# Gathers of rows as four plain 32-row loads, in a transformer block with all its gradients

## The chip, the cores and the metric

The kernel runs on one core of a Trainium2 chip. The metric is the device time of one execution in microseconds (us); the time before is the median of three runs. One further execution was recorded by the hardware profiler; its trace gives every duration below. TensorE is called PE, VectorE DVE, ScalarE ACT, GpSimd POOL; SP is the engine that only issues transfers.

## What is computed

One transformer block, forward and backward, at S = 2048 rows, D = 512, 32 heads of 16 columns and F = 1792, all in bfloat16. Attention is local and dilated: each row sees eight rows of its own past, two apart.

```python
def _A_ref(x, wqkv, wo):
    qkv = (x @ wqkv).reshape(B, S, 3, H, Dh).transpose(2, 0, 3, 1, 4)
    q, k, v = qkv[0], qkv[1], qkv[2]
    idx = pos[:, None] - (jnp.arange(8) * 2)[None, :]          # masked where < 0
    kg, vg = k[:, :, idx], v[:, :, idx]
    attn = _softmax(jnp.where(mask, einsum("bhsd,bhswd->bhsw", q, kg) * scale, -1e9))
    o = einsum("bhsw,bhswd->bhsd", attn, vg)
    return o.transpose(0, 2, 1, 3).reshape(B, S, D) @ wo
h  = x + _A_ref(_layernorm(x), wqkv, wo)
h2 = h + (_gelu(_layernorm(h) @ w1 + b1) @ w2 + b2)
out = h2, and the gradients of x, wqkv, wo, w1, b1, w2, b2 for grad_out
```

## The kernel before

The rows are worked in four chunks (`NC = 4`) of `CH = 512`. The forward pass goes through layer norm, the products with wqkv, attention, wo, a second layer norm and the two MLP products; then come the MLP's backward products, attention's backward pass chunk by chunk, and the weight gradients, which are dense matmuls that fill PE wherever they are placed.

Attention is not done with matmuls of q and k, as each row has eight partners only. Scores come from `dots` (product at L422): DVE multiplies q by the eight shifted copies of k, 128x4096 elements at a time (`prf` forward, `prb` backward), and PE sums over the head's columns (L430). What is weighted and summed over the eight partners goes through `band` (product at L449): DVE multiplies a tile `R` of fetched rows by coefficients `cf` (`prbo` for the output, `prbq`, `prbk` and `prbv` for the gradients), PE sums (L458) and ACT scales the result (L463). One `R` serves four such products.

`R` is filled by `gather` (L406, its transfer at L411): each of 128 partitions gets 18 rows of 512 numbers that lie in one piece in device memory, 18,432 bytes, and 2.36 MB in all. The rows come from `v_d`, `k_d`, `q_d` or `go_d`, where transposed copies of v, k, q and of the gradient of o were stored before. There are sixteen gathers: `Ro` of v for the forward pass, and `Rq` of k, `Rv` of go and `Rk` of q for the backward pass, each once a chunk. A gather is one indirect transfer on GpSimd's queue; the table `rowi`, written by eight small GpSimd instructions at L323, holds the index of each partition's first row. The same queue carries the stores of o and of the gradients of q, k and v (L266), the mask, and `rstd` (L346), a power taken for the layer norms.

The program is recorded as a list of operations by the class `Plan`; `op` derives from the tiles read and written what must come before what. `emit` then writes them in the sequence of the table `ORDER`, with each tile at the address in the table `HOMES`. Both tables are the result of a planner, which gave every operation a cost; the costs in the calls of `op` do nothing in the finished program. Each engine takes its instructions strictly in the order written. A tile can be loaded only when the tile that had its address is no longer read: in the backward pass `Rk`, `Rq` and `Rv` of one chunk can be issued only when the last product that reads the tile there has ended.

Three more places bear on the change. `consts` writes small constant matrices (`S32`, `Sum4`, `Pmat`, `Emat`), most on ACT. The layer norm of chunk 0 takes its root on ACT (L340, tile `ve`) and the reciprocal on DVE (L342). `warm` (L290) puts sixteen matmuls on a tile of zeros between PE's first products.

Of the kernel before, what the change touches and what calls it, by code (L numbers as in the profile page):

```python
# [10 lines left out]
P = 128  # L11
# [5 lines left out]
H = 32  # L17
# [131 lines left out]
def kernel(  # L149
# [43 lines left out]
    def cst(name, shape, dt=BF16):  # L193
# [8 lines left out]
    mhalf = cst("mhalf", [P, TPC], F32)  # L202
    epsc = cst("epsc", [P, 1], F32)
    zrow = cst("zrow", [RPAD, D])
    rowi = cst("rowi", [P, 2], mybir.dt.uint32)
# [28 lines left out]
    IDENT, PMAT, SUM4, NSUM4, S32B, SMB, IND8, EMAT, MKB, MHALF, ZROW, ROWI = (fx(n, None) for n in (  # L234
        "ident", "pmat", "sum4", "nsum4", "s32", "sm", "ind8", "emat", "mk", "mhalf", "zrow", "rowi"))
# [3 lines left out]
    EPSC = fx("epsc", epsc)  # L239
# [20 lines left out]
    def load(dst, ap, src_ap, kb, r=(), key=None, tag="load", soft=(), row=1, q="SP"):  # L260
        return op(q, 0.5, lambda: (SY if q == "SP" else A).dma_start(out=ap(), in_=src_ap()), r=r, w=[(dst, key)],
                  dma=kb / (DMA_RATE if row == 1 else WIDE_RATE), tag=tag, soft=soft, piece=0.006 + 0.0385 * row, mode=4)

    def store(dst, ap, src, src_ap, kb, key=None, skey=None, q="SP", tag="store", row=1):
        e, us = (SY, 0.45) if q == "SP" else (G, 0.6)
        return op(q, us, lambda: e.dma_start(out=ap(), in_=src_ap()), r=[(src, skey)], w=[(dst, key)] if dst is not None else (),  # L266
                  dma=kb / (DMA_RATE if row == 1 else WIDE_RATE), tag=tag, piece=0.006 + 0.0385 * row, mode=5)
# [14 lines left out]
    def warm(n):  # L282
# [8 lines left out]
        op("PE", 0.427 * n, mm, r=[z], w=[pz], tag="warm")  # L291

    def consts():
# [7 lines left out]
        op("ACT", 0.25, lambda: A.copy(out=_sub(Pmat[:], [[1, 8], [8, DH]]), in_=_sub(ident[:], [[DH, 8], [1, DH]])), r=[IDENT], w=[PMAT], tag="k")  # L301
        for j in range(4):
            op("ACT", 0.2, lambda j=j: A.copy(out=S32[32 * j:32 * j + 32, :], in_=ident[32 * j:32 * j + 32, 32 * j:32 * j + 32]),
               r=[IDENT], w=[(S32B, j)], tag="k")
# [10 lines left out]
        for g in range(4):  # L315
            op("ACT", 0.2, lambda g=g: A.copy(out=Emat[:, g, 8 * g:8 * g + 8], in_=ind8[:]), r=[IND8], w=[EMAT], tag="k")
# [88 lines left out]

    def gather(d_b, back, tag, soft=()):  # L406
        R = sb("R" + tag, [P, RW, 512])

        def g():
            t = d_b()  # L410
            G.indirect_dma_start(out=R().rearrange("p a d -> p (a d)"), out_offset=None,  # L411
                                 in_=_ap(t[0:1, :], [[RW * D, RB // RW], [1, RW * D]]),
                                 in_offset=bass.IndirectOffsetOnAxis(ap=rowi[:, int(back):int(back) + 1], axis=1),
                                 element_offset=(RPAD - 14 if back else 0) * D)
        op("POOL", 1.0, g, r=[d_b, ROWI], w=[R], dma=GATHER, tag="gather" + tag, soft=soft, piece=0.8, mode=4)
        return R
# [86 lines left out]
    wqk = sb("wqk", [P, DC, 2 * D])  # L503
    wv = sb("wv", [P, DC, D])
# [36 lines left out]
    def p1_proj(c, sel, dst, off, tag):  # L541
        for g2 in range(2):
            ps = ps_("psq" + tag, 2)
            for gg in range(2):
                g = 2 * g2 + gg

                for dcs in [range(DC)] if c in FM1 else [(0, 1), (2, 3)]:
                    def mm(g=g, gg=gg, ps=ps, dcs=dcs):
                        for dc in dcs:
                            T.matmul(ps()[:, gg * 512:(gg + 1) * 512], lhsT=wqk()[:, dc, sel * D + g * P:sel * D + (g + 1) * P],  # L550
                                     rhs=cols(st_[c]["ln1T"], dc, c in FM1), start=(dc == 0), stop=(dc == DC - 1))
                    op("PE", len(dcs) * MM, mm, r=[(wqk, sel), (st_[c]["ln1T"], None if c in FM1 else dcs[0] // 2)], w=[(ps, gg)], tag="qkv" + tag)
# [20 lines left out]
    def p1_qkv(c):  # L573
# [5 lines left out]
        else:  # L579
            kp = st_[c - 1]["kt"]  # L580
            op("DVE", 0.12, lambda: V.tensor_copy(out=kt()[:, :, 0:PAD], in_=kp()[:, :, CH:CH + PAD]), r=[(kp, 0), (kp, 1)], w=[(kt, "h")], tag="halo")
# [3 lines left out]
        to_tm_store(kt, PAD, k_d, c, True, "k", True)  # L585
        to_tm_store(qt, 0, q_d, c, False, "q", True)

    def p1_attn(c):
        d = st_[c]
        L = ps_("L", 2)  # L590
        dots(d["qt"], d["kt"], L, "f", lambda g: Emat[:, g, :], EMAT)
# [209 lines left out]
    def p3_go(c):  # L801
# [20 lines left out]
        to_tm_store(got, 0, go_d, c, False, "go", False)  # L822
# [175 lines left out]
    for i in (1, 0, 2):  # L998
        b = wv if i == 2 else wqk
        load(b, lambda b=b, i=i: b()[:, :, i % 2 * D:(i % 2 + 1) * D], lambda i=i: A_wqkv[:, i * D:(i + 1) * D].rearrange("(a p) j -> p a j", p=P), 512,  # L1000
             key=None if i == 2 else i, tag="wqkv")
    for c in range(1, NC):
# [106 lines left out]
FMB = ()  # L1109
LNK = 0  # L1110
# [167 lines left out]
```

## Time and profile before

| | us |
|---|---|
| three runs | 587.62, 597.37, 586.55 (median 587.62) |
| the profiled execution | 592.57 |
| its span | 590.8 |
| DVE busy | 494.9 |
| ACT busy | 379.1 |
| POOL busy | 45.7 |
| gathers, from issue to landing, median: Ro, Rq, Rv, Rk | 11.1, 10.7, 10.8, 11.8 |

The 1.8 us between span and time lie outside the recorded instructions. A row of the timeline gives the start and the length of a run of equal instructions, then engine, line, operation, the tiles written and read, and how many; in brackets stands how long the engine had been idle before and what ended that. `x4` in a row of 9 us is four instructions on end. PE's clock is shown as a share of full speed in each stretch; a matmul at half the clock takes twice as long and still counts as busy.

### The profile page before, as it was taken

What the parts mean: (1) busy time and instruction counts of PE and PEld (TensorE: products, weight loads), DVE (VectorE), ACT (ScalarE), POOL (GpSimd) and SP (SyncE); (2) the same over time, 40 slices, a digit from 0 to 9 for tenths busy, and PEclk for the clock granted to TensorE, in tenths of its full rate; (3) what the DMA queues carried; (4) which work ended last, traced back from release to release, by engine and by line L of the source; (5) the groups of instructions that cost most, each with busy time, mean ns of one, the idle gap of its engine ahead of it and who ended that gap; (6) DMA issues with size and microseconds to landing.
All of it is one profiled execution on the core that took longest, in us unless ns stands there. A gap on an engine that the chain in (4) does not pass through costs nothing. (4 is left out here: it accounts for less than half of the span.)

```text
span 590.8 us, 9131 instructions
## 1 busy us (share of the span) xinstructions
PE 555.7 (94%) x3526; PEld 265.3 (45%) x3580; DVE 494.9 (84%) x656; ACT 379.1 (64%) x549; POOL 45.7 (8%) x48
## 2 busy tenths in 40 slices
PE   3889997999999999999999999999999999969996
PEld 1444543455444444444444444455444444424442
DVE  7849979999999989959968878889989788768933
ACT  5878878999899973868913564552447743732622
POOL 1110021010000000000000200000110100701000
PEclk9989998999999999999999999999999999988999
DMA  8379886997642356469698998899989989274233
GB/s 262 103 235 299 239 316 178 289 206 223 159 120 78 99 148 184 116 136 225 132 182 166 197 195 211 256 285 227 312 278 263 311 256 349 66 313 161 63 99 98
DMA packets 160459, 118.68 MB, mean 201 GB/s; under 512 B 112480, under 2 KB 156064, under 8 KB 158368
## 3 DMA queue, kind: packets, MB, share of 16 engines
q1 hardware_dynamic: 157104, 76.68, 52.8%
q0 software_dynamic: 3312, 41.42, 19.4%
q8 instruction: 28, 0.46, 0.3%
q14 instruction: 15, 0.12, 0.1%
HBM read 55.74 MB, written 35.60 MB: 155 GB/s over the span
## 5 line engine op out<-in xcount | busy, mean ns | idle before, releaser
L779 PE MATMUL ps<-goT,w2T 128*128 128x512 bf16 x224 | 54.2, 379 | 0.0
L697 PE MATMUL ps<-ln2T,w 128*128 128x512 bf16 x224 | 52.6, 379 | 0.6 <-ACT xb L699 0.4
L793 PE MATMUL ps<-w1T,xb 128*128 128x512 bf16 x218 | 51.2, 379 | 0.3
L751 PE MATMUL ps<-w,gl 128*128 128x512 bf16 x218 | 50.5, 379 | 0.8 <-ACT gl L702 0.5
L781 DVE SCALAR_TENSOR_TENSOR xb<-xb,ps 128x512 bf16<-128x512 bf16 x56 | 37.0, 683 | 16.2 <-PE ps L779 11.6
L449 DVE TENSOR_TENSOR prbk<-Rk,cfk 128x4096 bf16<-128x4096 bf16 x16 | 35.8, 2287 | 14.5 <-issue 9.1
L907 PE MATMUL ps<-wqkvT,gqkvT 128*128 128x512 bf16 x187 | 45.8, 384 | 0.5 <-issue 0.3
L276 ACT CAST wgs<-ps 128x512 bf16<-128x512 f32 (+1 forms) x30 | 16.4, 558 | 46.5 <-PE ps L933 45.2
L699 ACT ACTIVATE xb<-ps,b1c 128x512 bf16<-128x512 f32 x56 | 35.9, 697 | 11.3 <-PE ps L697 8.5
L422 DVE TENSOR_TENSOR prb<-got,vw 128x4096 bf16<-128x4096 bf16 x16 | 36.1, 2282 | 7.8 <-PE ps L430 5.2
L933 PE MATMUL ps<-gw1in,ln 128*128 128x512 bf16 (+1 forms) x186 | 39.2, 352 | 0.3
L449 DVE TENSOR_TENSOR prbo<-Ro,cfo 128x4096 bf16<-128x4096 bf16 x16 | 36.0, 2282 | 3.6 <-DMA Ro<-v_d,rowi 3.6
L933 PE MATMUL ps<-gor,gw2in 128*128 128x512 bf16 x160 | 38.5, 379 | 0.5 <-issue 0.3
L276 ACT COPY gqkvT<-ps 128x1024 bf16<-128x1024 bf16 x24 | 23.8, 1014 | 20.2 <-PE ps L474 17.8
L422 DVE TENSOR_TENSOR prf<-qt,kt 128x4096 bf16<-128x4096 bf16 x16 | 35.8, 2276 | 1.1 <-ACT qt L276 1.1
L449 DVE TENSOR_TENSOR prbq<-Rq,cfq 128x4096 bf16<-128x4096 bf16 x16 | 35.7, 2282 | 1.1 <-PE ps L458 1.1
L449 DVE TENSOR_TENSOR prbv<-Rv,cfv 128x4096 bf16<-128x4096 bf16 x16 | 35.6, 2282 | 1.0 <-DMA Rv<-go_d,rowi 1.0
L933 PEld LDWEIGHTS <-ln 128*128 128x128 bf16 x256 | 24.4, 98 | 24.0 <-issue 2.5
L779 PEld LDWEIGHTS <-w2T 128*128 128x128 bf16 x224 | 21.8, 98 | 26.4 <-issue 0.4
L721 ACT ACTIVATE xb<-xb 128x2048 bf16<-128x2048 bf16 (+1 forms) x16 | 27.1, 1698 | 10.2 <-DVE xb L720 10.2
L793 PEld LDWEIGHTS <-xb 128*128 128x128 bf16 x224 | 21.8, 98 | 26.3 <-issue 0.2
L751 PEld LDWEIGHTS <-gl 128*128 128x128 bf16 x224 | 21.6, 98 | 26.5 <-ACT gl L702 1.2
(187 smaller groups left out, 1077.0 us busy)
## 6 DMA issues: line engine op xcount, KB each, us to landing
g_d<-gl SPq DMA_DIRECT2D x9, 512.0 KB, 4.6
gh_d<-xb SPq DMA_DIRECT2D x9, 512.0 KB, 3.4
w<-in_B_w_dram SPq DMA_DIRECT2D x2, 1792.0 KB
out_dram<-wgs SPq DMA_DIRECT2D x13, 256.0 KB, 4.7
xp<-in_A_x_dram SPq DMA_DIRECT2D x16, 128.0 KB, 3.6
ln_d<-ln SPq DMA_DIRECT2D x4, 512.0 KB, 6.2
gor<-in_grad_out_dram SPq DMA_DIRECT2D x16, 128.0 KB, 3.7
v_d<-tmv SPq DMA_DIRECT2D x8, 256.0 KB, 5.2
```

Of the source, the lines that this page charges most:

```text
L276: fn = lambda: A.copy(out=ap(), in_=pap())
L422: op("DVE", tt_us(4096), lambda g=g, pr=pr: V.tensor_tensor(out=pr(), in0=ql()[:, g, :].unsqueeze(1).to_broadcast([P, W, 512]), in1=_sub(k ...
L449: V.tensor_tensor(out=pr().rearrange("p a j (d h) -> p a j d h", h=H), in0=_sub(R()[:, o0, 0:1], [[st, 2], [512, 4], [32, DH], [1, H]]), i ...
L697: T.matmul(ps(), lhsT=w1()[:, dc, f * P:(f + 1) * P], rhs=cols(ln2T[c], dc, c in FM2), start=(dc == 0), stop=(dc == DC - 1))
L699: op("ACT", act_us(512, 1), lambda f=f, ps=ps, xb=xb, f0=f0: A.activation(out=xb()[:, f - f0, :], in_=ps(), func=ACT.Identity, bias=b1c[:, ...
L721: op("ACT", act_us(N), lambda xb=xb: A.activation(out=fl(xb), in_=fl(xb), func=ACT.Tanh, scale=GC), w=[xb], tag="tanh", mode=6)
L751: T.matmul(ps(), lhsT=d["g"][f // 4]()[:, f % 4, j * P:(j + 1) * P], rhs=w2()[:, f, :], start=(f == 0), stop=(f == FT - 1))
L779: T.matmul(ps(), lhsT=w2T()[:, dc, f * P:(f + 1) * P], rhs=cols(goT, dc, True), start=(dc == 0), stop=(dc == DC - 1))
L781: op("DVE", 0.61, lambda f=f, ps=ps, z=z, f0=f0: V.scalar_tensor_tensor(out=z()[:, f - f0, :], in0=z()[:, f - f0, :], scalar=1.0, in1=ps() ...
L793: T.matmul(ps(), lhsT=d["d"][f // 4]()[:, f % 4, j * P:(j + 1) * P], rhs=w1T()[:, f, :], start=(f == 0), stop=(f == FT - 1))
L907: T.matmul(ps(), lhsT=gT()[:, j, b * P:(b + 1) * P], rhs=wqkvT()[:, k0 + b, :], start=(i == 0 and b == 0), stop=(i == 2 and b == 3))
L933: T.matmul(ps()[:, 0:N], lhsT=l, rhs=r, start=(n == 0), stop=(n == k - 1))
```

## The change

In `gather`, the indirect transfer becomes four plain transfers of 32 partitions each, on the same queue. The source rows and the tile stay the same, so the table `rowi` and its eight instructions go. A product that reads the tile needs all four. In `consts`, ACT first takes the root of a constant, `sq0`, and the copies that make `Pmat`, `S32` and `Emat` come behind it, as they now read `sq0` as far as the planner sees; the ACT table loads fall from four to three. In `warm` the planner's cost alone is changed: the matmuls stay sixteen. Some options are added that are off (`QKP`, `TMD`). `ORDER` and `HOMES` are new from end to end: a new run of the planner over the changed list.

```diff
-        def g():
-            t = d_b()
-            G.indirect_dma_start(out=R().rearrange("p a d -> p (a d)"), out_offset=None,
-                                 in_=_ap(t[0:1, :], [[RW * D, RB // RW], [1, RW * D]]),
-                                 in_offset=bass.IndirectOffsetOnAxis(ap=rowi[:, int(back):int(back) + 1], axis=1),
-                                 element_offset=(RPAD - 14 if back else 0) * D)
-        op("POOL", 1.0, g, r=[d_b, ROWI], w=[R], dma=GATHER, tag="gather" + tag, soft=soft, piece=0.8, mode=4)
+        r0, dr = (RPAD - 2, -4) if back else (0, 4)
+        if GW == 4:
+            G_dma = lambda w: G.dma_start(out=R()[32 * w:32 * w + 32].rearrange("p a d -> p (a d)"), in_=_ap(d_b()[r0 + dr * w:r0 + dr * w + 1, :], [[16 * D, 32], [1, RW * D]]))
+            for w in range(4):
+                op("POOL", 0.58, lambda w=w: G_dma(w), r=[d_b], w=[(R, w)], dma=GATHER / 4, tag="gather" + tag, soft=soft, piece=0.8, mode=4)
...
-        op("PE", 0.427 * n, mm, r=[z], w=[pz], tag="warm")
+        op("PE", 0.2157 * n, mm, r=[z], w=[pz], tag="warm")
...
-        op("ACT", 0.25, lambda: A.copy(out=_sub(Pmat[:], [[1, 8], [8, DH]]), in_=_sub(ident[:], [[DH, 8], [1, DH]])), r=[IDENT], w=[PMAT], tag="k")
+        op("ACT", 0.25, lambda: A.activation(out=sq0[:], in_=epsc[:], func=ACT.Sqrt), r=[EPSC], w=[SQ0], tag="sd0", mode=7)
+        op("ACT", 0.25, lambda: A.copy(out=_sub(Pmat[:], [[1, 8], [8, DH]]), in_=_sub(ident[:], [[DH, 8], [1, DH]])), r=[IDENT, SQ0], w=[PMAT], tag="k")
...
-        for w4 in range(4):
-            for b_, o in ((0, 4 * w4), (1, 4 * (3 - w4))):
-                op("POOL", 0.12, lambda w4=w4, b_=b_, o=o: G.iota(rowi[32 * w4:32 * w4 + 32, b_:b_ + 1], pattern=[[0, 1]], base=o * D,
-                                                                 channel_multiplier=16 * D), w=[(ROWI, (w4, b_))], tag="k")
...
 ORDER = (
-    6, 14, 15, 13, 16, 7, 3, 17, 19, 20, 8, 5, 23, 24, 4, 0, 28, 11, 10, 82, 12, 2, 29, 35,
+    75, 6, 8, 11, 10, 5, 12, 24, 25, 26, 14, 42, 0, 7, 16, 3, 9, 60, 2, 52, 4, 48, 61, 62,
...
```

Three places of DVE's sequence show what the new tables do there. The numbers in a name are those of the tile's place in the list and its address; `st` and `mv` are a layer norm's statistics, `nm` its shift, `m` the maxima of the softmax, `jk` a dot product of the layer norm's backward pass (an `ISA` row, and one more that reads its sum), `gx` and `u` its results. Lines of the changed program lie 15 to 29 further down from the gather on (L449 is L464 there).

The first is DVE around the score products of chunk 0 and the maxima behind them. Before:

```order
L422 TENSOR_TENSOR prf_18_296<-qt_79_15_221,kt_19_3_123 128x4096
L581 COPY kt_121_18_303<-kt_19_3_123 128x4x16
L333 BN_STATS st<-xt_52_8_172 128x6
L334 BN_AGGR mv<-st 128x2
L422 TENSOR_TENSOR prf_19_308<-qt_79_15_221,kt_19_3_123 128x4096
L422 TENSOR_TENSOR prf_19_313<-qt_79_15_221,kt_19_3_123 128x4096
L422 TENSOR_TENSOR prf_20_315<-qt_79_15_221,kt_19_3_123 128x4096
L333 BN_STATS st<-xt_52_8_172 128x6
L334 BN_AGGR mv<-st 128x2
L344 TENSOR_SCALAR ve<-mv 128x4
L603 TENSOR_TENSOR m_153_18_409<-asb_16_401,ps 128x512
```

And now:

```order
L437 TENSOR_TENSOR prf_16_274<-qt_87_16_237,kt_0_1_99 128x4096
L346 SCALAR_TENSOR_TENSOR nm<-mv,rstd 128x4
L437 TENSOR_TENSOR prf_16_293<-qt_87_16_237,kt_0_1_99 128x4096
L437 TENSOR_TENSOR prf_17_296<-qt_87_16_237,kt_0_1_99 128x4096
L437 TENSOR_TENSOR prf_20_318<-qt_87_16_237,kt_0_1_99 128x4096
L330 BN_STATS st<-xt_78_14_222 128x6
L331 BN_AGGR mv<-st 128x2
L330 BN_STATS st<-xt_78_14_222 128x6
L331 BN_AGGR mv<-st 128x2
L330 BN_STATS st<-xt_78_14_222 128x6
L331 BN_AGGR mv<-st 128x2
L632 TENSOR_TENSOR m_148_17_394<-asb_16_382,ps 128x512
```

The four products `prf` now stand together, with one short `nm` between; the statistics of a tile that stood behind the first have moved away, and a third tile's statistics stand behind the last, ahead of `m`.

The second is DVE where the output products of the second `Ro` (`prbo`) meet the maxima of the next chunk's softmax (`m`). Before:

```order
L349 SCALAR_TENSOR_TENSOR nm<-mv,rstd 128x4
L449 TENSOR_TENSOR prbo_26_984<-Ro_28_820,cfo_26_957 128x4096
L603 TENSOR_TENSOR m_359_26_1014<-asb_25_1012,ps 128x512
L449 TENSOR_TENSOR prbo_26_1024<-Ro_28_820,cfo_26_957 128x4096
L605 TENSOR_TENSOR m_368_28_1030<-m_359_26_1014,m1h_27_1028 64x512
L449 TENSOR_TENSOR prbo_26_1034<-Ro_28_820,cfo_26_957 128x4096
L607 TENSOR_TENSOR m_382_23_1063<-m_368_28_1030,m2h_22_1061 32x512
L449 TENSOR_TENSOR prbo_22_1109<-Ro_28_820,cfo_26_957 128x4096
```

And now:

```order
L346 SCALAR_TENSOR_TENSOR nm<-mv,rstd 128x4
L632 TENSOR_TENSOR m_360_23_1009<-asb_22_1007,ps 128x512
L464 TENSOR_TENSOR prbo_22_1012<-Ro_29_867,cfo_21_974 128x4096
L634 TENSOR_TENSOR m_367_25_1023<-m_360_23_1009,m1h_24_1021 64x512
L464 TENSOR_TENSOR prbo_26_1044<-Ro_29_867,cfo_21_974 128x4096
L464 TENSOR_TENSOR prbo_24_1055<-Ro_29_867,cfo_21_974 128x4096
L636 TENSOR_TENSOR m_384_26_1065<-m_367_25_1023,m2h_25_1063 32x512
L464 TENSOR_TENSOR prbo_23_1073<-Ro_29_867,cfo_21_974 128x4096
```

The first `m` has moved from behind the first `prbo` to ahead of it; the last of the three stands behind the third product as before.

The third is DVE near the end of the backward pass, with the last product that reads one `Rq`, and `Rv` and `Rk` behind it. Before:

```order
L449 TENSOR_TENSOR prbq_36_4796<-Rq_35_4733,cfq_40_4424 128x4096
L1085 TENSOR_REDUCE gb_33_4855<-gb2p 128x4
L449 TENSOR_TENSOR prbv_34_4877<-Rv_33_4773,cfv_40_4352 128x4096
L449 TENSOR_TENSOR prbv_35_4898<-Rv_33_4773,cfv_40_4352 128x4096
L449 TENSOR_TENSOR prbv_35_4945<-Rv_33_4773,cfv_40_4352 128x4096
L449 TENSOR_TENSOR prbv_34_4970<-Rv_33_4773,cfv_40_4352 128x4096
L449 TENSOR_TENSOR prbk_34_4991<-Rk_36_4806,cfk_37_4520 128x4096
L449 TENSOR_TENSOR prbk_35_5011<-Rk_36_4806,cfk_37_4520 128x4096
L449 TENSOR_TENSOR prbk_35_5014<-Rk_36_4806,cfk_37_4520 128x4096
L495 ISA jk_1866_35_5041,sx<-gyr_1815_34_4857,ln1b_39_4540 128x512
L495 ISA sx 128x1
L449 TENSOR_TENSOR prbk_35_5043<-Rk_36_4806,cfk_37_4520 128x4096
```

And now:

```order
L464 TENSOR_TENSOR prbq_35_4825<-Rq_41_4694,cfq_40_4263 128x4096
L464 TENSOR_TENSOR prbv_33_4832<-Rv_41_4628,cfv_40_4428 128x4096
L510 ISA jk_1846_35_4878,sx<-gyr_1845_35_4876,ln1b_41_4539 128x512
L510 ISA sx 128x1
L510 ISA jk_1852_34_4894,sx<-gyr_1844_35_4874,ln1b_41_4539 128x512
L510 ISA sx 128x1
L464 TENSOR_TENSOR prbv_33_4951<-Rv_41_4628,cfv_40_4428 128x4096
L464 TENSOR_TENSOR prbv_34_4953<-Rv_41_4628,cfv_40_4428 128x4096
L464 TENSOR_TENSOR prbv_35_4966<-Rv_41_4628,cfv_40_4428 128x4096
L510 ISA jk_1875_34_4977,sx<-gyr_1845_35_4876,ln1b_41_4539 128x512
L510 ISA sx 128x1
L464 TENSOR_TENSOR prbk_36_4998<-Rk_33_4940,cfk_42_4681 128x4096
```

The products of `Rv` and `Rk` follow each other as before, but three `jk` now stand among or right behind the products of `Rv`, where there was none. On POOL's queue each gather's four parts stand together, but for one `Rv` near the end, whose last two parts stand behind all four of an `Rq`.

More of the change, by code (lines that the diff above doesn't have):

```diff
@@ L202 @@
     mhalf = cst("mhalf", [P, TPC], F32)
+    sq0 = cst("sq0", [P, 1], F32)
     epsc = cst("epsc", [P, 1], F32)
     zrow = cst("zrow", [RPAD, D])
[L205 removed]
     b1b = cst("b1b", [FT, P])
@@ L315, in consts @@
         for g in range(4):
-            op("ACT", 0.2, lambda g=g: A.copy(out=Emat[:, g, 8 * g:8 * g + 8], in_=ind8[:]), r=[IND8], w=[EMAT], tag="k")
+            op("ACT", 0.2, lambda g=g: A.copy(out=Emat[:, g, 8 * g:8 * g + 8], in_=ind8[:]), r=[IND8, SQ0], w=[EMAT], tag="k")
         op("POOL", 0.3, lambda: G.memset(mk[:], 0.0), w=[MKB], tag="k")
@@ L584, in p1_qkv @@
         p1_v(c)
-        to_tm_store(kt, PAD, k_d, c, True, "k", True)
-        to_tm_store(qt, 0, q_d, c, False, "q", True)
+        for fm, o, dd, back, n in ((kt, PAD, k_d, True, "k"), (qt, 0, q_d, False, "q")):
+            (tm_dma if (n, c) in TMD else to_tm_store)(fm, o, dd, c, back, n, c not in QKP)
     def p1_attn(c):
@@ L1001 @@
              key=None if i == 2 else i, tag="wqkv")
+    for i in (1, 0) if QKP else ():
+        op("POOL", 3.9, lambda i=i: G.tensor_copy(out=wqp()[:, :, i * D:(i + 1) * D].rearrange("p a (d h) -> p a d h", h=H),
+                                                  in_=_sub(wqk()[:, 0, 0:1], [[2 * D, DC], [1, DH], [DH, H]], i * D)), r=[(wqk, i)], w=[(wqp, i)], tag="hinwq")
     for c in range(1, NC):
@@ L1109 @@
 FMB = ()
+QKP = ()
+GW = 4
+TMD = ()
 LNK = 0
```

53 lines of the change are left out of this document (42 added, 11 removed), and 253 rows, old and new, of tables (HOMES, ORDER).

## The prediction

> **What bounds it now.** I read the page first: the busy shares and the slices.
>
> ```profile
> span 590.8 us, 9131 instructions
> PE 555.7 (94%) x3526; PEld 265.3 (45%) x3580; DVE 494.9 (84%) x656; ACT 379.1 (64%) x549; POOL 45.7 (8%) x48
> PE   3889997999999999999999999999999999969996
> PEclk9989998999999999999999999999999999988999
> ```
>
> PE is full nearly everywhere, and the change leaves its matmuls as they are. So what can be won is PE's idle time, 590.8 - 555.7 = 35.1 us, and the matmuls that run at a lower clock; the slices put both in the first sixth and in slices 36 and 37. What can be lost is not bounded in that way: DVE, at 84%, can become what PE waits for. The view of the waits then names what ends PE's idle time.
>
> ```profile
> PE ps L378 <- DVE ln L358: 8.6, 2, 7.7
> PE ps L458 <- DVE prbk L449: 6.8, 4, 3.0
> PE ps L400 <- ACT kt L276: 4.2, 1, 4.2
> PE ps L430 <- DVE prf L422: 2.7, 1, 2.7
> ```
>
> These four are 22.3 of the 35.1 us. The first is the start. The second is the late slices, where the timeline of the three engines, with POOL's rows first, shows the cause.
>
> ```profile
> 504.00 9.42 POOL L411 DMA_INDIRECT Rk<-q_d,rowi  x1 [11.83 <-DVE prbq L449]
> 513.73 0.94 POOL L411 DMA_INDIRECT Rv<-go_d,rowi  x1 [0.31 <-issue]
> 532.45 2.75 POOL L411 DMA_INDIRECT Rk<-q_d,rowi  x1 [17.78 <-DVE sx L495]
> ...
> 503.73 8.88 DVE L449 TENSOR_TENSOR prbv<-Rv,cfv 128x4096 bf16<-128x4096 bf16 x4
> 521.70 6.70 DVE L449 TENSOR_TENSOR prbk<-Rk,cfk 128x4096 bf16<-128x4096 bf16 x3 [9.09 <-issue]
> 528.32 0.68 DVE L495 CUSTOM_DVE_ANT_0 jk<-gyr,ln1b 128x512 bf16<-128x512 bf16 x1
> 532.10 6.69 DVE L449 TENSOR_TENSOR prbv<-Rv,cfv 128x4096 bf16<-128x4096 bf16 x3
> ...
> 526.25 0.61 PE L458 MATMUL ps<-prbk,S 128*32 128x512 bf16 x8 [3.00 <-DVE prbk L449]
> 528.45 1.89 PE L458 MATMUL ps<-prbk,S 128*32 128x512 bf16 x16 [1.59 <-DVE prbk L449]
> 531.39 1.04 PE L458 MATMUL ps<-prbk,S 128*32 128x512 bf16 x8 [1.04 <-DVE prbk L449]
> ```
>
> The issue of `Rk` takes 9.42 us, not the 0.94 of the next one. It begins 0.27 us into DVE's four `prbv` and ends at 513.42, 0.81 us behind their end at 512.61. The issue at 532.45 falls under the first of three `prbv` and lasts until 535.20, again 0.8 us behind that product's end (532.10 + 6.69 / 3 = 534.33). So while DVE runs such a product, the indirect issue stands still. The data then come late, DVE sits idle for 9.09 us, and PE waits three times, 5.63 us in all. A plain transfer on the same queue does not stand still: this store lies inside a run of such products.
>
> ```profile
> 425.77 0.58 POOL L266 DMA_DIRECT2D gv_d<-gvs  x1 [3.29 <-ACT gvs L463]
> ...
> 422.84 8.86 DVE L449 TENSOR_TENSOR prbq<-Rq,cfq 128x4096 bf16<-128x4096 bf16 x4
> ```
>
> [...]
>
> **The late bands.** The four issues of a gather take 4 x 0.58 = 2.3 us, 1.4 us more than 0.94, but start moving data after the first. With the stall gone, `Rk` at 504.00 would have been under way 8.5 us sooner, and DVE's 9.09 us would shrink to about one or two. In the new sequence the order of the parts here is `prbq`, four `prbv` with three `jk` among or behind them, then `prbk`; the parts of `Rk` can go out when the last `prbq` has ended, so DVE has 4 x 2.28 + 3 x 0.68, some 11 us of work before it needs them. The landing took this long:
>
> ```profile
> DMA to landing us min/median/max: 11.0/11.8/17.6
> ...
> 515.00:516.00 1.00, 1.00 (x18) 0.35 (x11) 0.00 (x0) 1.00 (x4) 0.00 (x0) 1.00 0.72 295
> ```
>
> (The first row is of the tile `Rk`; the second is the window from 515 to 516 us, with one gather alone in flight: clock 1.00, DMA share 0.72, 295 GB/s in the last column.) 11.8 us is the median, in which two of the four issues are stalled ones; against 11 us of work a wait of about one is left, which PE doesn't see if a matmul of the weight gradients stands there. The most to win is PE's 6.8 us on `prbk` and what the clock cost behind it:
>
> ```profile
> 30.00:32.00 2.00, 1.35 (x16) 0.50 (x15) 1.55 (x4) 0.13 (x1) 0.23 (x1) 0.54 1.13 225
> 32.00:34.00 2.00, 2.00 (x27) 1.50 (x20) 0.68 (x1) 0.89 (x2) 0.90 (x2) 0.61 0.42 78
> 532.00:534.00 2.00, 1.67 (x9) 0.58 (x5) 2.00 (x3) 0.64 (x2) 1.55 (x1) 0.50 0.00 0
> ```
>
> In these windows (PE's busy time second, the clock before the last two columns) a matmul behind an idle stretch runs at about half the clock: 532 to 534 alone loses 1.67 x 0.5 = 0.8 us, and I put 1.5 on the late place as a whole. Together 8.3 us; I take 7, as the last gathers stay tight, and keep 0 to 8.3.
>
> **Forward, the second gather.** Here is the third wait, followed upwards from PE.
>
> ```profile
> 85.99 2.29 DVE L449 TENSOR_TENSOR prbo<-Ro,cfo 128x4096 bf16<-128x4096 bf16 x1 [3.62 <-DMA Ro<-v_d,rowi]
> 88.20 0.68 DVE L603 TENSOR_TENSOR m<-asb,ps 128x512 bf16<-128x512 bf16 x1
> ...
> 88.91 0.62 ACT L604 COPY m1h<-m 64x512 bf16<-64x512 bf16 x1 [3.54 <-DVE m L603]
> 90.28 1.90 ACT L276 CAST kt<-ps 128x1024 bf16<-128x1024 f32 x2
> ...
> 92.23 1.01 PE L400 MATMUL ps<-Pmat,kt 128*128 128x128 bf16 x8 [4.24 <-ACT kt L276]
> ```
>
> `prbo` waited 3.62 us for `Ro`; `m` was queued behind it; ACT's `m1h` waited for `m`, and the cast of `kt`, which PE wanted, was queued behind `m1h`. In the new sequence `m` stands ahead of `prbo`, so a late `Ro` no longer holds up ACT. Gone are at most 4.24 us and, by the loss at 30 to 34 (1.35 x 0.46 + 2.00 x 0.39 = 1.4), the slow matmuls behind. I take 5 of these 5.6, since `Ro` may still be late for PE's own sums; the floor is 0.
>
> **The start.** ACT loads its table for the root when the first statistics are there already, and DVE waits for it; later DVE puts a tile's statistics between score products, and PE waits for the last of these.
>
> ```profile
> 4.77 1.28 ACT L340 ACT_TABLE_LOAD   x1
> 6.39 0.16 DVE L342 RECIPROCAL rstd<-ve 128x1 f32<-128x1 f32 x1 [1.58 <-ACT ve L340]
> 30.51 0.69 DVE L333 BATCH_NORM_STATS2 st<-xt 128x6 f32<-128x512 bf16 x1
> 33.32 0.69 DVE L603 TENSOR_TENSOR m<-asb,ps 128x512 bf16<-128x512 bf16 x1 [1.70 <-ACT asb L276]
> ...
> 30.65 1.90 PE L430 MATMUL ps<-prf,Emat 128*32 128x512 bf16 x16 [2.67 <-DVE prf L422]
> ```
>
> With the root first, that load lies beside the wait for the input. Of the 1.58 us some is used by the statistics (0.69 each) that follow it anyhow, so 0.9 is what I take (0 to 1.58). Without such statistics (0.69) between the products, the last `prf` ends 0.7 us sooner again. The three that now stand behind them, 3 x 0.69, fit into the 2.8 us from 30.51 until `m` begins, as `m` waits for PE and ACT anyhow. With 1.2 us of the 1.4 of slow clock, 2.8 us in all (0 to 4.1, which is PE's 2.67 and the 1.4). The zeros' matmuls stand earlier in PE's row; they are as many as before, and the wv products that now stand behind them fill the same time, so I cost the move at nothing; if that cover were thin, they would add at most the gap of 2.67 that they now shorten. The eight index instructions were on POOL, which is idle 92%.
>
> **What is added.** The new tables move every engine's row, and the plain issues are longer. A gather's last part goes out 1.4 us later; one `Rv` near the end has two of its parts queued behind four of an `Rq`, so it waits for that tile's address too; the power for `rstd` and the stores stand on the same queue. From 440 to 560 us DVE had this room:
>
> ```profile
> 440.00:480.00 40.00, 39.57 (x251) 18.33 (x253) 32.52 (x23) 25.38 (x39) 2.44 (x3) 1.00 0.97 287
> 480.00:520.00 40.00, 39.68 (x315) 19.72 (x320) 30.67 (x27) 22.71 (x42) 12.54 (x4) 1.00 0.63 222
> 520.00:560.00 40.00, 33.77 (x246) 16.00 (x249) 35.57 (x36) 16.73 (x37) 2.75 (x1) 0.91 0.45 167
> ```
>
> The fourth number is DVE's: 98.8 of 120 us, so 21.2 us of waiting can be borne there before DVE sets the end, if it is spread well. Eight gathers are used in this stretch: 1.4 x 8 = 11.2 fits. I put 1.5 us on waits that a new sequence brings, as much as the middle one of PE's three late waits, and keep 0 to 8, twice the longest of the waits above but the start's.
>
> The sum is -7 - 5 - 2.8 + 1.5 = -13.3 us. The profiled execution took 592.57, so it would take 579.3; the median of the runs is 587.62, 4.95 below the profiled one, and the same step from it gives **574.3 us**.
>
> **Rivals.** First, 32 rows land later than 128. Nearest are these two loads of 128 KB, the first into 32 partitions, the second into 128:
>
> ```profile
> xp<-in_A_x_dram SPq DMA_DIRECT2D x16, 128.0 KB, 3.6
> xt<-in_A_x_dram SPq DMA_DIRECT2D x4, 128.0 KB, 2.2
> ```
>
> 1.4 us more for 128 KB; other traffic was on at the time, so it is a hint only. If the data land 3 us later in all, eight gathers make DVE wait 24 us, just what the room holds: the late gain is lost, the early ones stay, and with the 1.5 us of new waits it ends at 587.62 - 5 - 2.8 + 1.5 = 581.3. Second, on the other side: the parts move at half the rate, one after another. The 2.36 MB took 8.0 us at 295 GB/s; 8 us more make a landing of 19.8 against 11 of work, so 8 x 8.8 - 21.2 = 49 us of DVE's time would be set on the end. That is the far end; it decides from 21.2 / 8 = 2.7 us beyond the cover, and halfway, with transfers of two gathers side by side, DVE waits some 5 us at each, 8 x 5 - 21.2 = 19 us; without the late gain, 581.3 + 19 = 600. For it speaks that every part fills a quarter of the partitions; against it, that four parts are queued at once.
>
> [...]
>
> Third, the change does not do what the first part says: the stall is not of the index but of any load on that queue under DVE's products (the 0.58 was a store). Then four issues stand still where one did, the late gain does not come and some new waits do, and it ends near 583, between the first rival and the time before.
>
> **Chances.** About 2% is what a measurement of this kernel can tell from no change; the lines lie at 575.9 and 599.4. My forecast has 0.58, and its own range goes from 565 to 583: at the low end all terms at full size (-18, so 569.6) and 5 us more, as the new sequence may also fill some of the 12.8 us of PE's idle time outside the four rows; at the high end half of the gains and 3 us of new waits. About three quarters of that chance, 0.44, I put under the lower line, as its middle lies there and unlooked-for filling is on that side too; 0.14 is above. Landing some 3 us later has 0.15, the stall that stays 0.05, both within 2%. The half rate has 0.22, of which I put 0.18 past the upper line, and a sequence that fits badly adds 0.03 from the others. So faster 0.44, within 2% 0.35, slower 0.21. The range is 565 to 602: it leaves out most of the half rate's upper side, some 0.14, and 0.04 below.
>
> **What would show it.** Right: `Rk`'s issues near 500 us at 0.6 us each under `prbv`; DVE's idle time ahead of `prbk` under 3 us; no wait of PE on `kt` near 90 us; the reciprocal's wait under 0.7. Wrong: `R` tiles landing later than 14 us, with DVE waiting for `Rq`, `Rv` or `Rk` throughout 440 to 560; or plain issues of over 2 us. The number would also be wrong if a wait opens at a place that has none now, such as ACT's sinks.

## The result

The changed kernel takes 658.8 us (median of four runs, 647.91 to 671.93) against 587.85 us. The ratio is 1.109, with a 95% interval of 1.095 to 1.123; two of the four runs were disturbed on the chip, and ratios, here and below, leave such runs out. The forecast was 574.3 us with a range of 565 to 602: wrong in sign.

The page of the changed kernel, in the same parts as before: busy times, PE's slices and clock, and the software queue, on which the gathers run.

```profile
span 646.1 us, 9285 instructions
PE 576.7 (89%) x3580; PEld 267.4 (41%) x3580; DVE 497.7 (77%) x656; ACT 379.2 (59%) x549; POOL 50.9 (8%) x88
PE   5897799879999999999999999939839999599797
PEclk9898989989999999999999999968959998799799
q0 software_dynamic: 4080, 41.42, 27.7%
```

The same row of the kernel before:

```profile
q0 software_dynamic: 3312, 41.42, 19.4%
```

(Packets, MB, share of sixteen engines' span.) DVE, ACT and PE do the same work (PE's weight loads are 3580 in both; the trace of before lacks 54 records of matmuls). PE is idle for 646.1 - 576.7 = 69.4 us, 34.3 more than before, and busy for 21.0 more, as its clock drops more often (a mean of 0.951 against 0.988, so 0.049 x 646.1 = 31.6 us of clock are lost instead of 7.1). The third row is the cause in small: the same 41.42 MB keep the engines of transfer busy for 27.7% of 646.1 = 179 us instead of 115. The waits of PE and of DVE show where that comes out.

```profile
PE ps L962 <- DMA gw1in<-gh_d: 10.3, 1, 10.3
PE ps L473 <- DVE prbk L464: 10.2, 4, 4.2
PE ps L936 <- ACT gqs L478: 8.9, 1, 8.9
PE ps L473 <- DVE prbo L464: 7.7, 5, 3.8
PE ps L375 <- DVE ln L355: 6.7, 1, 6.7
PE ps L962 <- DMA ln1b<-ln_d: 6.6, 1, 6.6
PE ps L648 <- ACT e L642: 3.7, 1, 3.7
PE ps L489 <- DVE st L330: 3.3, 1, 3.3
PE ps L290 <- ACT kt L276: 2.0, 1, 2.0
```

```profile
DVE prbk L464 <- DMA Rk<-q_d: 19.5, 4, 9.1
DVE prbq L464 <- DMA Rq<-k_d: 10.0, 3, 5.4
DVE prbv L464 <- DMA Rv<-go_d: 8.9, 1, 8.9
DVE prbo L464 <- DMA Ro<-v_d: 5.7, 1, 5.7
```

DVE now waits 44.1 us for gathers; before it was 10.0 us, and 9.1 more behind the stalled issue. And PE waits for two transfers that are no gathers: the transposed load of `gw1in`, 10.3 us, and `ln1b`, 6.6 us. For `gw1in`, SP's issues show where the time goes (duration in ns, shortest, median and longest; before, then now):

```profile
L270 SPq DMA_TRANSPOSE gw1in<-gh_d x12: 1268/2530/8757, 248.3 to 443.8; - x12
```

```profile
L270 SPq DMA_TRANSPOSE gw1in<-gh_d x12: 1260/2416/23812, 265.9 to 493.6; - x12
```

The longest issue stands for 23.8 us where it stood for 8.8 before. `ln1b` is less clear: the median landing of its loads is as before (9.0 us against 9.2), the last two are issued only at 544.06 and 545.35 us, and PE goes on at 557.54, so a late issue and a slow landing can both have a part in it. Of the two waits that the forecast meant to remove in the forward pass and at the start's end, those on `kt` at the table products and on `prf` are gone; but PE now waits 2.0 us for a `kt` ahead of the zeros' matmuls (L290). The stall is gone as well; here are the last three gathers on POOL, then DVE around the first of them.

```profile
558.30 1.93 POOL L425 DMA_DIRECT2D Rk<-q_d  x4 [20.44 <-DMA out_dram<-wgso]
570.28 1.93 POOL L425 DMA_DIRECT2D Rv<-go_d  x4 [10.05 <-DVE prbv L464]
581.86 1.93 POOL L425 DMA_DIRECT2D Rk<-q_d  x4 [9.64 <-DVE prbk L464]
...
557.74 2.29 DVE L464 TENSOR_TENSOR prbv<-Rv,cfv 128x4096 bf16<-128x4096 bf16 x1
563.29 6.70 DVE L464 TENSOR_TENSOR prbv<-Rv,cfv 128x4096 bf16<-128x4096 bf16 x3 [2.04 <-PE ps L473]
572.05 4.50 DVE L464 TENSOR_TENSOR prbk<-Rk,cfk 128x4096 bf16<-128x4096 bf16 x2 [1.45 <-DMA Rk<-q_d]
```

All four issues of a gather take 1.93 us, under products that held one indirect issue for 9.42. But `Rk`, issued from 558.30 on, is there only at about 572.0: 13.7 us, where the indirect gathers took 10 to 12. And in the stretch in which most is lost, the windows read, before and then now:

```profile
380.00:440.00 60.00, 58.32 (x435) 29.89 (x442) 55.50 (x34) 26.66 (x40) 5.02 (x6) 1.00 0.98 273
440.00:500.00 60.00, 59.46 (x399) 28.20 (x404) 50.58 (x43) 34.82 (x55) 4.63 (x5) 1.00 0.93 290
```

```profile
380.00:440.00 60.00, 48.57 (x335) 23.81 (x332) 43.34 (x26) 20.31 (x27) 5.72 (x12) 0.89 1.08 191
440.00:500.00 60.00, 46.94 (x320) 20.22 (x319) 37.68 (x24) 25.01 (x38) 7.08 (x15) 0.89 1.06 234
560.00:570.00 10.00, 10.00 (x83) 4.77 (x82) 7.96 (x9) 4.40 (x9) 0.23 (x1) 0.87 0.99 221
```

The last three numbers are clock, share of the transfer engines and GB/s. From 380 to 500 us the engines' share is 1.06 to 1.08 at 191 to 234 GB/s, where they moved 273 to 290 at 0.93 to 0.98. The last window holds one gather and hardly anything else: with it the engines' share is 0.99 at 221 GB/s. One indirect gather alone moved 295 GB/s at a share of 0.72 in the one microsecond that the prediction shows; from 514 to 522 us, which is that gather and the beginning of the next, the window reads 386 GB/s at 1.01.

### The profile page after: what moved, and what is told of

Same layout as the page of the kernel before. It is cut to its first block, busy times and chain, and to the rows that moved or that the text cites. A ratio compares the mean times of both kernels' runs of the same rounds, so it can differ in the third digit from the quotient of the medians.

```text
span 646.1 us, 9285 instructions
## 1 busy us (share of the span) xinstructions
PE 576.7 (89%) x3580; PEld 267.4 (41%) x3580; DVE 497.7 (77%) x656; ACT 379.2 (59%) x549; POOL 50.9 (8%) x88
## 3 DMA queue, kind: packets, MB, share of 16 engines
q0 software_dynamic: 4080, 41.42, 27.7%
## 4 chain that ended last, share of the span: by engine, by line
PE 48%; DMA 23%; DVE 13%; issue 6%; SPq 4%; ACT 3%; POOL 2%; DVEq 0%; POOLq 0%; ACTq 0%
PE ps L962 11%; PE ps L808 7%; PE ps L780 6%; PE ps L726 6%; PE ps L822 6%; DMA Rk<-q_d 5%; DMA out_dram<-wgs 4%; DMA Ro<-v_d 4%; PE ps L936 3%; SPq L261 2%; PE ps L473 2%; DMA Rq<-k_d 2%; DVE prbk L464 2%; DVE prbo L464 2%; DVE prbq L464 2%
## 5 line engine op out<-in xcount | busy, mean ns | idle before, releaser
L936 PE MATMUL ps<-wqkvT,gqkvT 128*128 128x512 bf16 x192 | 51.1, 410 | 8.9 <-ACT gqs L478 8.9
L962 PE MATMUL ps<-gw1in,ln 128*128 128x512 bf16 (+1 forms) x192 | 42.6, 370 | 10.3 <-DMA gw1in<-gh_d 10.3
L464 DVE TENSOR_TENSOR prbk<-Rk,cfk 128x4096 bf16<-128x4096 bf16 x16 | 35.8, 2285 | 19.5 <-DMA Rk<-q_d 19.5
L276 ACT COPY gqkvT<-ps 128x1024 bf16<-128x1024 bf16 x24 | 24.1, 1015 | 44.9 <-PE ps L489 34.3
L464 DVE TENSOR_TENSOR prbq<-Rq,cfq 128x4096 bf16<-128x4096 bf16 x16 | 35.7, 2283 | 13.8 <-DMA Rq<-k_d 10.0
L464 DVE TENSOR_TENSOR prbv<-Rv,cfv 128x4096 bf16<-128x4096 bf16 x16 | 35.8, 2286 | 13.6 <-DMA Rv<-go_d 8.9
L464 DVE TENSOR_TENSOR prbo<-Ro,cfo 128x4096 bf16<-128x4096 bf16 x16 | 36.0, 2283 | 9.8 <-DMA Ro<-v_d 5.7
L962 PE MATMUL ps<-gor,gw2in 128*128 128x512 bf16 x168 | 40.4, 380 | 0.0
L936 PEld LDWEIGHTS <-gqkvT 128*128 128x128 bf16 x192 | 19.0, 103 | 35.3 <-issue 17.7
```

Of the source, the lines that this page charges most:

```text
L276: fn = lambda: A.copy(out=ap(), in_=pap())
L464: V.tensor_tensor(out=pr().rearrange("p a j (d h) -> p a j d h", h=H), in0=_sub(R()[:, o0, 0:1], [[st, 2], [512, 4], [32, DH], [1, H]]), i ...
L936: T.matmul(ps(), lhsT=gT()[:, j, b * P:(b + 1) * P], rhs=wqkvT()[:, k0 + b, :], start=(i == 0 and b == 0), stop=(i == 2 and b == 3))
L962: T.matmul(ps()[:, 0:N], lhsT=l, rhs=r, start=(n == 0), stop=(n == k - 1))
```

## The experiments

The traces also hold a record of each packet. A gather is 128 packets of 18,432 bytes, one row for each partition. The table gives, for the gathers that an experiment changes, the mean time of such a packet, the median time from the first packet's start to the last one's end, and the ratio to the kernel before on the same chip.

| kernel | a gather is | us a row | us a gather | ratio (95%) |
|---|---|---|---|---|
| before | 1 indirect | 0.82 | 7.8 | 1 |
| after | 4 x 32 next to each other | 1.32 | 12.3 | 1.109 (1.095 to 1.123) |
| e1 | new order, 1 indirect | 0.79 | 7.6 | 1.009 (1.004 to 1.013) |
| e2 | 4 x 32, old order | 1.44 | 12.5 | 1.120 (1.112 to 1.129) |
| e3 | 4 x 32, eight gathers | 1.33 | 12.5 | 1.049 (1.039 to 1.060) |
| e4 | 4 x 32 on every 4th partition, eight | 2.23 | 23.6 | none (725 us) |
| e5 | 1 x 128, eight | 1.25 | 27.7 | 1.287 (1.269 to 1.306) |
| e6 | 2 x 64, eight | 1.28 | 29.0 | 1.289 (1.271 to 1.308) |
| e7 | 8 x 16, eight | 2.07 | 20.1 | 1.182 (1.161 to 1.203) |
| e8 | 4 x 32, the last four | 1.35 | 12.5 | 1.011 (1.001 to 1.022) |
| e9 | 16 x 8 on every 4th partition | 0.82 | 15.2 | 1.164 (1.147 to 1.181) |
| e10 | 16 x 8 next to each other | 1.76 | 35.3 | 1.630 (1.610 to 1.649) |
| e11 | 4 x 32, the first four of q and go | 1.32 | 12.5 | none (597 to 639 us) |
| e12 | new order, as e9 | 0.80 | 14.7 | 1.174 (1.160 to 1.188) |

**The order or the loads.** The first three kernels take the change apart (all edits from here on are shown shortened: `...` and conditions in words stand for the rest): the new order without the new loads, and the new loads without the new order, for all gathers and for the eight of q and go.

```diff
  # e1: open in the new order, at the place of the fourth part
- G.dma_start(out=R()[32 * w:32 * w + 32]..., in_=_ap(d_b()[r0 + dr * w:...], [[16 * D, 32], [1, RW * D]]))
+ if w is the last: G.indirect_dma_start(...as before...)
  # e2: in the old order, in the place of the indirect transfer; e3: the same if not back
- G.indirect_dma_start(...)
+ for w in range(4): G.dma_start(out=R()[32 * w:32 * w + 32]..., in_=_ap(..., [[16 * D, 32], [1, RW * D]]))
```

> The changed kernel with its new order, but each gather is one indirect transfer again, issued where the fourth part stood. Theory A, the 32-row loads move their bytes more slowly and hold up the other transfers too: near the time before, 575 to 595 us, landings back to 10 to 12 us, the transfers of the software queue back to some 115 us of sixteen engines. Theory B, the new order is bad by itself: 630 us or more, with landings as short as before and PE still idle for 60 us.

Measured: 594.89 us.

> The kernel before in its old order, with each indirect gather replaced in place by four plain loads of 32 neighbouring partitions. Theory A: most of the loss is here too, 620 to 660 us. Theory B: 578 to 592 us, as the issues no longer stall.

Measured: 660.49 us, as much as the whole change. (The trace, and with it the row's 1.44 us, is of its longest run, 690.78 us.)

> As the one before, but only the eight gathers of q and go (Rk and Rv) are four loads of 32 neighbouring partitions; those of v and k stay indirect. Theory A: about half of the loss, 598 to 625 us; a gather alone in flight moves some 225 GB/s and lands in 13 to 14 us from its first issue. Theory B: 578 to 592 us.

Measured: 614.97 us. So the loss is in the loads; the order and the early root, with indirect gathers, cost 0.9%. PE's waits in e1 say why they win nothing:

```profile
PE ps L381 <- DVE ln L361: 6.9, 1, 6.9
PE ps L488 <- DVE prbo L479: 3.2, 1, 3.2
PE ps L977 <- DMA ln1b<-ln_d: 3.1, 1, 3.1
PE ps L663 <- ACT e L657: 2.9, 1, 2.9
PE ps L504 <- ACT ost L493: 2.2, 1, 2.2
PE ps L291 <- ACT kt L277: 1.6, 1, 1.6
```

The waits on `kt` at the table products (4.2), on `prf` (2.7) and `prbk` (6.8) are gone, and the start is 0.8 us shorter; but the five waits below the first row have come, 13.0 us together, and PE is idle for 592.4 - 557.6 = 34.8 us, as long as before (35.1).

**What about the loads is slow.** Next, only how a gather is cut was changed, in the old order: into fewer and wider loads, into more and narrower ones, and with the partitions of a load apart or together. The gathers of v and k run backwards from partition group to group (`dr = -4`), which one load can't express, so the wider ones were tried on those of q and go.

```diff
+ # e4
+ for w in range(4): G.dma_start(out=R()[w:P:4]..., in_=_ap(d_b()[16 * w:...], [[4 * D, 4], [64 * D, 8], [1, RW * D]]))
+ # e5
+ G.dma_start(out=R()..., in_=_ap(d_b()[0:1, :], [[4 * D, 4], [16 * D, 32], [1, RW * D]]))
+ # e6
+ for w in range(2): G.dma_start(out=R()[64 * w:64 * w + 64]..., in_=_ap(d_b()[8 * w:...], [[4 * D, 2], [16 * D, 32], [1, RW * D]]))
+ # e7
+ for w in range(8): G.dma_start(out=R()[16 * w:16 * w + 16]..., in_=_ap(..., [[16 * D, 16], [1, RW * D]]))
```

> The same eight gathers as four loads of 32 rows each, but every load goes to every fourth partition, so that it spans all 128. Bytes, rows and issues are those of the run with 32 neighbouring partitions. Theory A in its form that where the partitions lie sets the rate: 576 to 588 us, some 295 GB/s alone in flight, landing in 9 to 11 us. Theory C, that four small loads in place of one cost by their number: the same time as with neighbouring partitions, 598 us or more.

Measured: 725.04 us (693.1 to 751.2), for which no ratio was taken; 2.23 us a row. Neither theory had that: spreading a load over all partitions made it worse. The run doesn't tell partitions from source, since its source pattern got a third dimension.

> Old order; each of the eight gathers of q and go (Rk, Rv) is one plain load into all 128 partitions, those of v and k stay indirect. Theory A (what counts is how many partitions one load spans): a row of 18,432 bytes takes 0.7 us as in the indirect gathers, a gather alone 7 to 8 us, and as the issues no longer stall the kernel takes 576 to 588 us. Theory C (a plain load from this queue is slower than an indirect one, whatever its width): a row takes 1.3 us, 598 us or more.

Measured: 760.16 us. Theory A fails. A row takes 1.25 us, as theory C has it, but theory C doesn't say why the gather takes 27.7. From 128 x 1.25 / 27.7, some 6 rows are under way at a time, where the indirect gather has 128 x 0.82 / 7.8 = 13.

> The same eight gathers as two loads of 64 neighbouring partitions. [...] Theory A with a rate in proportion to the width, or theory C by the number of loads: some 1.0 us a row, 9 to 10 us a gather, 595 to 605 us.

Measured: 760.19 us, the same again; a row takes 1.28 us and a gather 29.0, not 9 to 10. What e4 to e6 share is the third dimension of the source pattern. In e5 and e6 some 6 rows are under way at a time (128 x 1.28 / 29.0 = 5.6 in e6) instead of 13; e4, with four loads, has 128 x 2.23 / 23.6 = 12, so e4 is slow by the row and not by their number. What sets either was not shown: which engine a packet ran on is not in the trace.

> The same eight gathers as eight loads of 16 neighbouring partitions. [...] Theory C, by the number of loads alone: 1.3 us a row and 4 issues more, 1 to 2 us a gather more than with four loads, 615 to 635 us.

Measured: 696.9 us, 2.07 us a row and 20.1 a gather. Theory C had 1.3 us a row and 615 to 635 us, so the number of loads alone does not account for it. The clean test is the next pair, with equal loads in number, rows, bytes and dimensions; as to the tile, only the partitions differ: a load of e9 goes to every fourth one of 32, a load of e10 to eight next to each other.

```diff
+ # e9
+ for b4 in range(4):
+     for w in (0, 2, 1, 3):
+         G.dma_start(out=R()[32 * w + b4:32 * w + 32:4]..., in_=_ap(d_b()[r0 + dr * w + 16 * b4:...], [[64 * D, 8], [1, RW * D]]))
+ # e10: out=R()[32 * w + 8 * b4:32 * w + 8 * b4 + 8], in_=_ap(d_b()[r0 + dr * w + 128 * b4:...], [[16 * D, 8], [1, RW * D]])
```

> Old order; each of the sixteen gathers is sixteen plain loads of eight rows, each load to every fourth partition of 32, and loads to the lower and the upper 64 partitions take turns. [...] If the cost were in the number of loads, or in a plain load as such: 1.3 us a row or more, 13 us a gather or more, 650 us or more.

Measured: 696.05 us. A row takes 0.82 us, as in the indirect gather and not 1.3 or more, so a plain load as such is not slow by the row; but a gather takes 15.2 us, and that and the kernel's time are what was expected of a cost in the number of loads, 13 us and 650 us or more.

> [...] Bytes, rows, issues and turns are those of the run with spread partitions. [...] If the partitions did not matter: the same time as with spread partitions.

Measured: 965.95 us, where e9 took 696.05; 1.76 us a row (1.2 to 2.3 from gather to gather), 35.3 a gather. The software queue's row of the two, e9 first:

```profile
q0 software_dynamic: 9200, 41.44, 17.1%
```

```profile
q0 software_dynamic: 9200, 41.44, 25.0%
```

Equal packets and bytes; with a span of 699.4 and 965.1 us that is 120 and 241 us of the sixteen engines. The step between rows in the source differs too (64 rows against 16), so strictly the pair shows the two together; but 32 neighbouring rows with a step of 16 in the source take 1.33 us, so a step of 16 alone is not what gives 1.76. In e9 the rows are fast, and a gather is slow because few of them are under way at a time: 128 x 0.82 / 15.2 = 7. By the packet records never more than 8 are, the rows of one load, where the indirect gathers have up to 19: so two whole loads did not run side by side. GpSimd, which issues sixteen loads a gather, is also busy for 149.7 us instead of 45.7, and the stores and `rstd` stand on the same queue.

> The changed kernel's order with the sixteen spread loads of eight rows, issued where the fourth part stood. [...] If the new order has a fault of its own: 595 us or more, as with the indirect gathers in this order.

```diff
  # e12: the loads of e9 at the place of the fourth part, in the changed kernel
```

Measured: 700.64 us; in the new order the same.

**Late or in the way.** Slow rows can cost in two ways: the products wait for them, or other transfers do.

```diff
  # e8 and e11, old order: four loads of 32 rows for some gathers of q and go, the others indirect
+ if any(d_b is x for x in (q_d[2], q_d[3], go_d[2], go_d[3])):   # e8; e11: [0] and [1]
  # e14, old order, behind the indirect transfer
+ if not back:
+     for _ in range(2): G.dma_start(out=<scratch in device memory>, in_=_ap(t[0:1, :], [[16 * D, 32], [1, RW * D]]))
```

> Old order; only the last four gathers of q and go (from 490 us on, where the other transfers leave the engines half idle) are four loads of 32 partitions. If what costs is the time to landing, which the products wait for: about 4.5 us for each, 598 to 610 us. If what costs is that the transfers crowd the others out, it costs little here, and the stall of 9.4 us is gone: 580 to 592 us.

Measured: 595.74 us, ratio 1.011, between the two.

> Old order; only the first four gathers of q and go (390 to 475 us, where the other transfers keep the engines busy) are four loads of 32 partitions; the last four stay indirect, with their stall. If crowding out is what costs: 606 to 622 us, with waits for other transfers. If the products' wait for the landing is what costs: 4.5 us each at most, and less where there is cover, 592 to 606 us.

Measured: 610.07 us with a spread from 597.2 to 638.92, and 587.1 to 602.96 for the kernel before on that chip: inconclusive.

> The kernel before, and behind each of the eight indirect gathers of q and go two copies of 0.59 MB from device memory to device memory on the same queue (results unused): they take up the transfer engines for some 4 us a gather, as the 32-row loads did, but come behind the gather, whose landing they do not delay. If the 32-row loads cost by crowding the other transfers out: most of what the eight 32-row gathers cost, 605 to 620 us. If they cost by landing later: 587 to 597 us.

Measured: 610.29 us, ratio 1.026 (1.014 to 1.039), though every gather is indirect and its rows take 0.8 us. PE's waits of that run include

```profile
PE ps L937 <- DMA gw1in<-gh_d: 7.3, 1, 7.3
```

the same transposed load that is waited for in the changed kernel. So the copies cost some 15 us (0.026 x 588) for 22 us more of the sixteen engines (22.4% of 610.2 against 19.4% of 590.8). That is not crowding alone: the next gathers stand behind the copies in the queue, one `Rq` landed after 22.6 us, and DVE waits for `Rq`, which it did not before:

```profile
DVE prbq L453 <- DMA Rq<-k_d,rowi: 9.6, 2, 8.2
```

On the other side e9 has no more engine time in its gathers than before (0.82 us a row in both), lands them late (15.2 us a gather against 7.8), and loses 16%, though its issues also fill GpSimd's queue. And in e8, at the end, where the engines' share is 0.79 (500 to 560 us), DVE waits for the tiles:

```profile
DVE prbk L453 <- DMA Rk<-q_d: 7.0, 2, 4.1
DVE prbv L453 <- DMA Rv<-go_d: 6.0, 2, 3.3
```

Both ways cost; how the 60 us of the changed kernel divide between them stays open.

**The stall, and the early terms.** Two runs keep the indirect gathers and the old order, and take away single waits.

```diff
  # e13, in band(), ahead of the first of four products
+ if R is an Rv of chunk 2 or 3:
+     for _ in range(3):
+         V.tensor_reduce(out=gap[:], in_=Sm[:], axis=mybir.AxisListType.X, op=ALU.add)
  # e15: e13, and
+ A.activation(out=gap[:, 0:1], in_=ident[:, 0:1], func=ACT.Sqrt)     # first on ACT
+ _o.remove(392); _o.insert(_o.index(254) + 1, 392)                    # the second Ro's first product behind m
```

> The kernel before with its indirect gathers and its order; in the two places late in the backward pass where a stalled issue of Rk falls under the products prbv, DVE first sums a constant matrix three times (one SBUF input, some 1.8 us in all, result unused). If the issue stands still because DVE reads two SBUF inputs: both issues of Rk take about 1 us instead of 9.4 and 2.8, DVE waits 1 to 3 us instead of 9.1 before prbk, and the kernel takes 580 to 586 us. If the issue is slow there for another reason, or the stall costs nothing in the end: 587 to 592 us.

Measured: 586.78 us, ratio 0.997 (0.993 to 1.001). POOL, then DVE, in that run:

```profile
508.80 0.94 POOL L412 DMA_INDIRECT Rk<-q_d,rowi  x1 [11.83 <-DVE prbq L454]
519.72 2.74 POOL L412 DMA_INDIRECT Rv<-go_d,rowi  x1 [9.98 <-DVE prbv L454]
530.10 0.93 POOL L412 DMA_INDIRECT Rk<-q_d,rowi  x1 [7.65 <-DVE sx L500]
...
508.52 2.12 DVE L453 TENSOR_REDUCE gap<-Sm 128x4 f32<-128x512 bf16 x3
510.56 8.89 DVE L454 TENSOR_TENSOR prbv<-Rv,cfv 128x4096 bf16<-128x4096 bf16 x4
519.36 6.69 DVE L454 TENSOR_TENSOR prbk<-Rk,cfk 128x4096 bf16<-128x4096 bf16 x3
```

Both issues of `Rk` take 0.94 us while DVE reads one matrix, and `prbk` follows with hardly a wait. The `Rv` between them, which has no such gap, now takes 2.74 under `prbk`. That is the stall shown by taking the product away from under the issue; that the second input is what counts in the product was not tested by itself. The time, though, moved by less than can be told from nothing.

> As the run with the three sums ahead of prbv, and two of the changed kernel's other steps done alone in the old order: ACT takes a root of a constant first, and the first m of the next softmax stands ahead of the first product of the second Ro. By the forecast's own terms the start gives 0.9 us and the forward place 4 to 5: 574 to 581 us, PE's wait of 4.2 us on kt gone. If these waits move elsewhere: 581 to 588 us.

Measured: 584.80 us, ratio 0.991 (0.986 to 0.995): faster than both kernels, than the one before by some 5 us. PE's timeline, with the rows that answer to those of before:

```profile
6.36 0.39 PE L386 MATMUL ps<-ident,ln 128*128 128x128 bf16 x2 [6.36 <-DVE ln L366]
30.25 1.47 PE L438 MATMUL ps<-prf,Emat 128*32 128x512 bf16 x16 [2.67 <-DVE prf L430]
87.98 0.61 PE L408 MATMUL ps<-Pmat,kt 128*128 128x128 bf16 x8 [0.73 <-ACT kt L278]
90.32 1.05 PE L470 MATMUL ps<-prbo,S 128*32 128x512 bf16 x16 [1.73 <-DVE prbo L461]
93.18 1.01 PE L623 MATMUL ps<-m,nSum 32*128 32x512 bf16 x2 [1.81 <-DVE m L619]
```

PE starts 1.35 us sooner (6.36 against 7.71), but reaches the score sums only 0.4 us sooner (30.25 against 30.65), as the products there are DVE's own chain, and the statistics between them stand where they stood. The wait on `kt` falls from 4.24 to 0.73, and 1.73 for `prbo` and 1.81 for `m` come right behind it. The POOL row of `Rk` shows what that leaves: issued at 463.62 where it was at 463.23 before.

```profile
463.62 0.94 POOL L419 DMA_INDIRECT Rk<-q_d,rowi  x1 [20.29 <-DVE prbq L461]
504.39 0.94 POOL L419 DMA_INDIRECT Rk<-q_d,rowi  x1 [11.83 <-DVE prbq L461]
```

So up to there nothing was won, and the span's 8.4 us less (582.4 against 590.8, one profiled execution each) come from behind it, where the stall was. The trace of e13 says the same: from the issue of the `Rk` that had stalled to the end are 590.8 - 504.00 = 86.8 us before, 586.8 - 508.80 = 78.0 in e13 and 582.4 - 504.39 = 78.0 in e15; e13 comes to that issue 4.8 us later than before, though its edit acts only from there on.

## Why the prediction was wrong

**The step that failed** is the landing in the late bands: "11.8 us is the median ... against 11 us of work a wait of about one is left". That took the indirect gather's transfer for that of the four loads and added issue time alone. The transfer is another: 12.3 us instead of 7.8, as many rows under way (128 x 1.32 / 12.3 = 13.7), but 1.32 us a row instead of 0.82. `Rk` near 558 us was there after 13.7 us, and DVE waited 44.1 us for gathers in all. e2 has it without the new order and loses 12.0%; e1 has the order without it and loses 0.9%.

**The rival that came true, too cheap.** The half rate stood among the rivals with a chance of 0.22 and a price of 600 us; that the four loads move their bytes more slowly was right, at 7.8 / 12.3 = 0.63 of the rate and not at half: 4.5 us more a gather where the rival had 8. A row takes 0.82 us in loads of 8 spread partitions (e9), 1.32 of 32 neighbouring ones, 2.07 of 16 (e7) and 1.76 of 8 (e10). What makes them slow was not shown: e9 and e10 differ in the source step too, and the loads of e4 and e5 reach over all 128 partitions and take 2.23 and 1.25. The weight the rival was given was too small: the only row against it was that four parts are queued at once, and this was no evidence that they run side by side: at no time are more than 20 rows of a gather under way in the changed kernel, where one part has 32. The price was too small for three reasons. It counted DVE's room for eight gathers from 440 us on; all sixteen pay, and PE lost most from 380 to 500 (60 - 48.57 and 60 - 46.94 us idle, against 1.7 and 0.5 before). It counted a late landing only, and put nothing on other transfers, while the engines were busy for 64 us more: PE waited 10.3 us for `gw1in`, and in e14 copies behind the gathers, with the late landings that they bring, cost 2.6%. (Of the 6.6 us for `ln1b`, the loads' part is not known: e1 has 3.1 us of that wait without them.) And the clock was low around PE's longest waits (0.51 from 426 to 440 and from 470 to 484 us, where PE waits for `gw1in` and `gqs`): 21.0 us more busy time for the same matmuls.

**The stall** was read rightly: an indirect issue stands still under DVE's products (9.42 us under `prbv`) and a plain one doesn't (1.93 us for four), and e13 shows that it hangs on the product (0.94 us without one). Its size is unsettled: 7 us were put on it; the traces of e13 and e15 are both 8.8 us shorter behind that place, but over their runs e13 is 0.3% faster, with an interval that holds no change, and e15 5 us in all.

**The start and the forward place** were right as waits and wrong as time. In the changed kernel and in e1 the waits on `prf` and on `kt` at the table products are gone, as forecast; e15 gains 1.35 us at the first matmul (0.9 was put on it). In e1, PE comes to the two small matmuls behind the score sums (`ident`, `mk`) at 30.22 us against 32.48, so most of the 2.8 us was there at that point, in spite of 1.57 us in which the zeros' matmuls, moved forward, wait for `kt`; the prediction had put that move at nothing and named the doubt. In the whole time the terms of 2.8 and 5 us do not show: other waits took their place, in e15 at 90 us those for `prbo` and `m`. The prediction did not ask what is late next there. The 1.5 us put on new waits of a new order were too little: e1 has 13.0 us of them on PE.

**The third rival**, that a plain load stalls as well, is out: at 558.30 us the four issues of `Rk` took 1.93 us under `prbv`.

## What to carry to other kernels

Before a transfer is replaced by another form, ask for the time of one row and for how many rows are under way, not for its bytes: the same 2.36 MB took 7.8 to 35 us here, depending on the partitions that one load covers and on how it is cut. Ask for the transfer engines' extra time as well, and not for the consumer's wait alone: here their share was 1.06 to 1.08 from 380 to 500 us, the slower gathers took 64 us more of them, and PE waited 10.3 us for a transposed load on another queue; how the two divide was not settled. And look for issues that stand still under another engine's work: the indirect issue took 9.42 us under VectorE's products, and in e13 2.12 us of other work on VectorE in front of them let it through in 0.94, with no change of the transfer; the gain in time was too small here to be told from nothing.

## What was not expected of the hardware

One load of 128 rows and two of 64 were the slowest of the wide forms, 27.7 and 29.0 us a gather against 12.5 for four of 32: here wider was not faster. Sixteen loads of eight spread rows moved each row as fast as the indirect gather (0.82 us) and still took 15.2 us a gather. And copies whose results nothing reads, 22 us of the sixteen engines, cost some 15 us of a kernel whose PE was busy 94% of the time, in part by the gathers that landed late behind them.
